# A small load moved to the head of the ACT queue, x moved to GpSimd, and the layer-norm transposes moved into those of K0

## Chip, cores, metric

One core of one Trainium2 chip. The metric is the device time of one execution in microseconds (us), lower is better. Executions of one kernel on one core are compared within rounds on the same chip; all runs quoted here are of the fast state unless said otherwise. A ratio is the mean time of one kernel's fast runs over that of the other's of the same rounds, so it is not quite the ratio of the medians that are quoted. Under 2% of difference counts as "same"; the 95% interval is given where smaller differences matter.

## The reference

A decode step: layer norm of x (2 x 576), attention over a sliding window of 2048 cached positions (32 query heads, 16 key/value heads of 128), plus a squared-ReLU MLP (576 to 4608 to 576), all added to x.

```python
x  = A_x                                    # 2 x 1 x 576, bf16
xn = _layernorm(x, axis=-1)
return x + _A_ref(xn, A_k_cache, A_v_cache, A_wq, A_wo) \
         + _B_ref(xn, B_w1, B_b1, B_w2, B_b2)
# _A_ref: q = xn @ wq; softmax(q k^T / sqrt(128)) v over the last 2048 positions; @ wo
# _B_ref: relu(xn @ w1 + b1)**2 @ w2 + b2
```

The arithmetic is small. The work is to bring 53.6 MB of K, V and weights into SBUF.

## The kernel before

All large loads are issued by the Sync engine (SP) in one queue, K0 first, then wq, then K and V blocks of 2 MB that rotate through six buffers. TensorE transposes each K block in eight groups of four matmuls; VectorE and ScalarE copy the results out in turn.

```python
x_sb = const.tile([B, D], BF16, name="x_sb")
nc.scalar.dma_start(out=x_sb[:], in_=x2d)                # x: 2 rows of 1152 B, ACT queue
# ... constants; an activation that loads the table ...
for f in issue_kv(k_tiles, A_k_cache, 0, "k"):           # K0: 128 partitions x 16 KB, SP queue
    f()
for i in range(NW):
    issue_wq(i)
# ... identity; layer norm of x_sb into xn_sb and xr_sb on VectorE and ScalarE ...
pro_ps = psum.tile([P, NXN, B], BF16, tag="misc", name="pro_ps")
for c in range(NFULL):
    pe_tr(out=pro_ps[:, c, :], in_=xn_sb[:, c:NFULL * P:NFULL], identity=ident[:B, :B])
for sg in range(S):
    pe_tr(out=pro_ps[:, NFULL + sg, :], in_=xr_sb[:, sg, :], identity=ident[:B, :B])
xnT = const.tile([P, NXN, B], BF16, name="xnT")
nc.vector.tensor_copy(out=xnT[:], in_=pro_ps[:])         # six transposes, then one copy
# ... (cut)
for g in range(NG):
    transposes(0, g)                                      # K0
for c in range(KC):
    q_block(c)                                            # uses xnT and wq
# ... scores, softmax; b1 and later b2 by GpSimd:
b2_sb = const.tile([1, D], BF16, name="b2_sb")
nc.gpsimd.dma_start(out=b2_sb[:], in_=B_b2.rearrange("(o n) -> o n", o=1))
```

## Time and profile before

| | before |
|---|---|
| time, median of 3 first runs (range) | 134.68 us (134.64 to 134.70) |
| span in the profile | 132.7 us |
| busy share TensorE / VectorE / ScalarE / GpSimd | 70% / 46% / 35% / 6% |
| bytes on the SP queue | 53.61 MB of 53.74 |
| first packet of K0; last landing of the last weights | 2.15 us; 129.19 us |

How to read it: a row of digits is the busy share of the span in 40 slices, 9 being 90% or more. "Packet records" and "landing records" below are the trace's single DMA packets and the semaphore counts they raise; the numbers in the text that no shown line carries come from there. The lines themselves are in the prediction.

### The profile page before, as it was taken

How to read it: one execution, taken by the hardware profiler on the slowest of the kernel's cores; microseconds unless marked ns; L12 is line 12 of the kernel's file. 1: busy time of each engine (PE TensorE's matmuls, PEld its weight loads, DVE VectorE, ACT ScalarE, POOL GpSimd, SP SyncE). 2: the span in 40 equal slices, each digit the busy share in tenths (PEclk: the TensorE clock that was granted, in tenths of full speed). 3: DMA queues.
4: the chain of work that ended last, by engine and by line, in shares of the span. 5: the costliest groups of instructions: out<-in, count | busy, mean ns of one | idle time of the engine just before them, and what ended most of it. 6: DMA issues, size and time to landing. Idle time of an engine off the chain costs nothing.

```text
span 132.7 us, 2060 instructions
## 1 busy us (share of the span) xinstructions
PE 92.7 (70%) x838; PEld 55.9 (42%) x838; DVE 61.2 (46%) x169; ACT 46.3 (35%) x63; POOL 7.5 (6%) x21
## 2 busy tenths in 40 slices
PE   0069456897499689688787629959937985556960
PEld 0058222673456355444444325524515942313640
DVE  6914304346533872863764772287041436443010
ACT  5717301494343274175175043412040661000010
POOL 7500000100100100100100100010000001000000
PEclk9999977779769999999999995995995599655896
DMA  4999999999999999999999999999999999999940
GB/s 159 396 412 449 415 444 415 439 420 430 437 420 444 415 449 415 439 425 434 425 415 449 420 435 433 427 433 444 417 425 430 430 434 439 406 425 434 414 203 1
DMA packets 4268, 53.74 MB, mean 405 GB/s; under 512 B 542, under 2 KB 544, under 8 KB 1060
## 3 DMA queue, kind: packets, MB, share of 16 engines
q1 hardware_dynamic: 4184, 53.61, 95.0%
q8 instruction: 6, 0.10, 0.3%
q0 software_dynamic: 64, 0.01, 0.0%
q14 instruction: 2, 0.02, 0.0%
q10 hardware_dynamic: 12, 0.00, 0.0%
HBM read 53.62 MB, written 0.00 MB: 404 GB/s over the span
## 4 chain that ended last, share of the span: by engine, by line
DMA 88%; PE 7%; SPq 3%; issue 0%; DVE 0%; DVEq 0%
DMA k<-in_A_k_cache_dram 67%; DMA w<-in_B_w_dram 21%; PE kT_ps L93 4%; SPq L111 1%; PE pv_ps L90 1%; SPq L118 1%; PE sc_ps L90 1%; SPq L123 0%; PE tail_ps L90 0%; DVE fin_sb L550 0%; PE sm L90 0%; DVEq L550 0%
## 5 line engine op out<-in xcount | busy, mean ns | idle before, releaser
L93 PE MATMUL kT_ps<-ident_f,k 128*128 128x128 f32 x256 | 43.7, 322 | 6.6 <-DMA k<-in_A_k_cache_dram 4.9
L297 ACT COPY kT<-kT_ps 128x1024 bf16<-128x1024 bf16 x32 | 31.8, 1012 | 30.1 <-PE kT_ps L93 30.1
L93 PEld LDWEIGHTS kT_ps<-ident_f,k 128*128 128x128 f32 x256 | 34.3, 165 | 18.6 <-issue 6.6
L299 DVE COPY kT<-kT_ps 128x1024 bf16<-128x1024 bf16 x32 | 22.0, 686 | 29.9 <-PE kT_ps L93 29.1
L90 PE MATMUL sc_ps<-kT,qz 128*32 128x512 bf16 x128 | 9.7, 383 | 6.2 <-DVE kT L299 5.5
L90 PE MATMUL pv_ps<-v,pT 128*32 128x512 bf16 x128 | 13.5, 467 | 0.0
L330 ACT ACTIVATE pr<-sc_ps,nb 128x512 bf16<-128x512 f32 x8 | 5.5, 687 | 20.7 <-DVE nb L327 20.7
L323 POOL PARTITION_ALL_REDUCE gmax<-m x8 | 2.9, 364 | 102.7 <-DVE m L321 80.4
L368 DVE SCALAR_TENSOR_TENSOR acc<-pv_ps,f,acc 128x128 f32<-128x128 f32 x24 | 8.3, 346 | 0.5
L90 PE MATMUL sm<-acc,tohead 128*64 128x128 f32 x16 | 4.2, 352 | 5.8 <-DVE acc L368 5.5
L332 DVE STREAM_TRANSPOSE pT<-pr 128x512 bf16<-128x512 bf16 x8 | 5.7, 709 | 5.2 <-ACT pr L330 5.2
L90 PE MATMUL out_ps<-wo,ws 128*2 128x288 bf16 x64 | 6.7, 390 | 1.1 <-DVE ws L390 1.1
L319 DVE TENSOR_REDUCE mx<-sc_ps 128x1 f32<-128x512 f32 x8 | 5.5, 692 | 3.4 <-PE sc_ps L90 3.0
L90 PEld LDWEIGHTS <-qz 128*32 128x32 bf16 x128 | 2.0, 94 | 10.0 <-DVE kT L299 7.1
L544 ACT COPY part<-out_ps 2x144 f32<-2x144 f32 x2 | 0.5, 268 | 15.0 <-DVE part L544 14.9
L90 PEld LDWEIGHTS <-ws 128*2 128x2 bf16 x64 | 3.7, 114 | 4.6 <-DVE ws L390 1.5
L90 PE MATMUL sm<-sums,samec 128*128 128x1 f32 x16 | 3.3, 276 | 3.1 <-DVE od L386 3.1
L90 PEld LDWEIGHTS sm<-acc,tohead 128*64 128x64 f32 x16 | 1.8, 161 | 8.6 <-DVE acc L368 7.9
L90 PEld LDWEIGHTS <-xnT 128*2 128x2 bf16 x100 | 2.6, 87 | 6.7 <-issue 5.5
L90 PEld LDWEIGHTS <-pT 128*32 128x32 bf16 x128 | 3.3, 102 | 4.3 <-issue 4.0
L90 PE MATMUL q_ps<-wq,xnT 128*2 128x512 bf16 x32 | 2.9, 499 | 3.2 <-DMA wq<-in_A_wq_dram 3.2
L93 PE MATMUL pro_ps<-ident,xn_sb 2*128 2x2 bf16 x4 | 0.3, 172 | 6.7 <-DVE xn_sb L198 6.7
(86 smaller groups left out, 62.3 us busy)
## 6 DMA issues: line engine op xcount, KB each, us to landing
k<-in_A_k_cache_dram SPq DMA_DIRECT2D x8, 2048.0 KB, 22.0
v<-in_A_v_cache_dram SPq DMA_DIRECT2D x8, 2048.0 KB, 27.0
wo<-in_A_wo_dram SPq DMA_DIRECT2D x2, 2304.0 KB, 23.4
w<-in_B_w_dram SPq DMA_DIRECT2D x2, 2304.0 KB, 30.9
wq<-in_A_wq_dram SPq DMA_DIRECT2D x2, 2048.0 KB, 13.9
w<-in_B_w_dram SPq DMA_DIRECT2D x3, 1296.0 KB, 27.7
w<-in_B_w_dram SPq DMA_DIRECT2D x1, 1008.0 KB, 31.8
w_rem<-in_B_w_dram SPq DMA_DIRECT2D x1, 576.0 KB, 34.2
```

What stands on the lines that cost most here:

```text
L90: return tc.keep_in_program_order(nc.tensor.matmul(out, **kw))
L93: return tc.keep_in_program_order(nc.tensor.transpose(**kw))
L111: return [lambda i=i: nc.sync.dma_start(out=tl[:, i * n:(i + 1) * n], in_=v[:, :, i * n:(i + 1) * n]) for i in range(parts)]
L118: nc.sync.dma_start(out=tl[:, 0:RW * width], in_=rows[:, i * RW * width:(i + 1) * RW * width])
L297: nc.scalar.copy(out=dst, in_=src)
L299: nc.vector.tensor_copy(out=dst, in_=src)
L319: nc.vector.tensor_reduce(out=mx[:], in_=sc_ps, axis=AX.X, op=ALU.max)
L323: nc.gpsimd.partition_all_reduce(gmax[:], m2[:], channels=P, reduce_op=ReduceOp.max)
L330: nc.scalar.activation(out=pr[:], in_=sc_ps, func=ACT.Exp, bias=nb[:], scale=scale, accum_out=sums[:])
L332: nc.vector.transpose(out=pT[:].rearrange("p t m -> p (t m)"), in_=pr[:])
L368: op = nc.vector.scalar_tensor_tensor(out=nx[:], in0=pv_ps[:, j, :], scalar=f[:, j:j + 1], in1=acc[:], op0=ALU.mult, op1=ALU.add)
L544: cp(out=part[32 * i:32 * i + B, :], in_=out_ps[32 * (i // 2):32 * (i // 2) + B, (i % 2) * OQ:(i % 2 + 1) * OQ])
```

## The change

Three moves, meant together: b2 becomes the first load on the ACT queue, in a view of 16 pieces so as to run on all 16 DMA engines; x, which had that place, goes to GpSimd, whose queue the page calls software_dynamic (software descriptors, SWDGE); since x then lands later, the six transposes of the normalised x move from ahead of K0's transposes to the middle of them.

```diff
+    b2_sb = const.tile([1, D], BF16, name="b2_sb")
+    nc.scalar.dma_start(out=b2_sb[:].rearrange("o (k n) -> o k n", k=16),
+                        in_=B_b2.rearrange("(o k n) -> o k n", o=1, k=16))
     x_sb = const.tile([B, D], BF16, name="x_sb")
-    nc.scalar.dma_start(out=x_sb[:], in_=x2d)
+    nc.gpsimd.dma_start(out=x_sb[:], in_=x2d)
 ...
-    pro_ps = ...  six pe_tr ...  xnT copy          # (before all K0 transposes)
 ...
-    for g in range(NG):
+    for g in range(NG // 2):
+        transposes(0, g)
+    pro_ps = ...  six pe_tr ...  xnT copy
+    for g in range(NG // 2, NG):
         transposes(0, g)
 ...
-    b2_sb = const.tile([1, D], BF16, name="b2_sb")
-    nc.gpsimd.dma_start(out=b2_sb[:], in_=B_b2.rearrange("(o n) -> o n", o=1))
```

More of the change, by code (lines that the diff above doesn't have):

```diff
@@ L156, in issue_w2 @@
         w2_tiles[(g, r0)] = tl
+    b2_sb = const.tile([1, D], BF16, name="b2_sb")
+    nc.scalar.dma_start(out=b2_sb[:].rearrange("o (k n) -> o k n", k=16), in_=B_b2.rearrange("(o k n) -> o k n", o=1, k=16))
     x_sb = const.tile([B, D], BF16, name="x_sb")
-    nc.scalar.dma_start(out=x_sb[:], in_=x2d)
+    nc.gpsimd.dma_start(out=x_sb[:], in_=x2d)
     eps_t = const.tile([B, 1], F32, name="eps_t")
@@ L203 @@
         nc.vector.tensor_copy(out=xr_sb[:, sg, sg::S], in_=xn_sb[:, NFULL * P:D])
-    pro_ps = psum.tile([P, NXN, B], BF16, tag="misc", name="pro_ps")
-    for c in range(NFULL):
-        pe_tr(out=pro_ps[:, c, :], in_=xn_sb[:, c:NFULL * P:NFULL], identity=ident[:B, :B])
-    for sg in range(S):
-        pe_tr(out=pro_ps[:, NFULL + sg, :], in_=xr_sb[:, sg, :], identity=ident[:B, :B])
-    xnT = const.tile([P, NXN, B], BF16, name="xnT")
-    nc.vector.tensor_copy(out=xnT[:], in_=pro_ps[:])
     own = const.tile([P, NC], F32, name="own")
@@ L490, in step @@
         softmax(u)
-    for g in range(NG):
+    for g in range(NG // 2):
+        transposes(0, g)
+    pro_ps = psum.tile([P, NXN, B], BF16, tag="misc", name="pro_ps")
+    for c in range(NFULL):
+        pe_tr(out=pro_ps[:, c, :], in_=xn_sb[:, c:NFULL * P:NFULL], identity=ident[:B, :B])
+    for sg in range(S):
+        pe_tr(out=pro_ps[:, NFULL + sg, :], in_=xr_sb[:, sg, :], identity=ident[:B, :B])
+    xnT = const.tile([P, NXN, B], BF16, name="xnT")
+    nc.vector.tensor_copy(out=xnT[:], in_=pro_ps[:])
+    for g in range(NG // 2, NG):
         transposes(0, g)
```

## The prediction

> **What bounds the kernel now.** I read the page top down first: busy shares, the slices, the queue table, the chain that ended last.
>
> ```profile
> span 132.7 us, 2060 instructions
> PE 92.7 (70%) x838; PEld 55.9 (42%) x838; DVE 61.2 (46%) x169; ACT 46.3 (35%) x63; POOL 7.5 (6%) x21
> ...
> DMA  4999999999999999999999999999999999999940
> ...
> q1 hardware_dynamic: 4184, 53.61, 95.0%
> ...
> DMA 88%; PE 7%; SPq 3%; issue 0%; DVE 0%; DVEq 0%
> ```
>
> No compute engine is above 70%, while the 16 DMA engines stand at 9 in every slice from the second to the last but two. One queue, that of the Sync engine, carries 53.61 of the 53.74 MB, and the chain is DMA for 88% of the span. Next the stretches view says at what rate that queue runs (columns: stretch, its length, busy time and instructions of each engine, granted clock, DMA share, GB/s):
>
> ```profile
> 14.00:100.00 86.00, 65.33 (x587) 37.25 (x579) 42.87 (x106) 32.92 (x46) 2.55 (x7) 0.90 1.01 430
> 100.00:127.00 27.00, 19.89 (x173) 12.62 (x173) 9.37 (x28) 4.83 (x6) 0.36 (x1) 0.68 1.00 425
> 127.00:129.00 2.00, 1.10 (x40) 0.69 (x35) 0.60 (x2) 0.54 (x2) 0.00 (x0) 1.00 0.39 158
> ```
>
> 430 GB/s in the middle, 425 later, so the stream is steady, then a ragged end. The 2 MB of one K or V block take about 4.87 us at 430 GB/s. The landing records put the 16 completions of the last weight piece between 127.33 and 129.19 us: the DMA engines end up to 1.86 us apart, and the slowest decides. The end of the chain in order of time, and the timeline there:
>
> ```profile
> 101.64 27.55 DMA w<-in_B_w_dram
> 129.19 0.04 issue
> 129.23 0.32 PE tail_ps L90 x8
> ...
> 129.65 0.31 DVE fin_sb L550
> ```
>
> So the time is: when the stream starts (first packet of K0 at 2.15 us in the packet records), plus 127.0 us of stream to 129.19, plus 3.5 us of tail to the end of the span at 132.7, plus about 2 us outside the span (134.68 measured). A change matters only if it moves one of these. Everything it touches lies at the beginning, so the last view is the timeline of the first 15 us (start, duration, engine, line, operation, idle time before and its releaser):
>
> ```profile
> 0.73 0.65 SPq L111 DMA_DIRECT2D k<-in_A_k_cache_dram  x1
> 0.73 0.56 ACTq L159 DMA_DIRECT2D x_sb<-in_A_x_dram  x1
> ...
> 1.78 0.85 POOL L501 DMA_DIRECT2D b_sb<-in_B_b_dram  x1
> ...
> 2.64 0.53 POOL L506 DMA_DIRECT2D b_sb<-in_B_b_dram  x1
> ...
> 6.66 0.29 PE L93 MATMUL pro_ps<-ident,xn_sb 2*128 2x2 bf16 x4 [6.66 <-DVE xn_sb L198]
> ...
> 8.42 3.74 PE L93 MATMUL kT_ps<-ident_f,k 128*128 128x128 f32 x20 [1.25 <-DMA k<-in_A_k_cache_dram]
> ...
> 13.95 0.54 SPq L111 DMA_DIRECT2D v<-in_A_v_cache_dram  x1
> 18.08 1.88 PE L90 MATMUL q_ps<-wq,xnT 128*2 128x512 bf16 x16 [3.20 <-DMA wq<-in_A_wq_dram]
> ```
>
> The reader should see that x, b1, b2 and the layer norm are all finished before K0 lands (8.37 us), that TensorE then works until about 14.9 and idles 3.2 us for the second half of wq.
>
> **What the Trainium skill says.** (1) "DMA: Bandwidth & Descriptors", section "Why a DMA increments its semaphore by 16 and not by 1": a copy runs on the largest number k up to 16 that divides the slowest dimension of both sides, on hardware queues the lowest-numbered k engines; on a software queue all 16 post the completion. The trace agrees: x (2 rows) left two packets of 1152 B and two of 4 B on the ACT queue. It explains the intent, because b2 viewed as 16 pieces of 36 values gets k = 16. (2) Same page, "Issuing engines are not separate DMA queues": whoever issues, the same 16 DMA engines do the work. So moving x and b2 frees no bandwidth; the 100% DMA share in the stretches agrees. (3) Same page, "Latency and other measured facts": first byte after about 0.6 us by hardware descriptors, about 1 us by software. Here x's first packet came 0.93 us after its issue began, but b1's 4.39 us after (6.17 against 1.78) behind a full stream, and b1 and b2 landed 6.4 and 6.3 us after issue. The measured 6.3 is what I use for x. (4) "SBUF — State Buffer", section "SBUF: two separate sides": some VectorE modes keep GpSimd from writing software descriptors. x's descriptors will be written at about 0.7 to 1.6 us, while VectorE does its memsets. The b1 issue took 0.85 us against 0.53 for b2, which may or may not be that; it can delay x by tenths.
>
> **The change part by part.**
>
> *b2 from GpSimd to the head of ACT.* 1152 B. In the packet records b2 was already 16 data packets of 72 B at about 12 ns; the bytes and their spread over engines stay. GpSimd loses an issue of 0.53 us that nobody waited for. ACT keeps one issue, 0.56 us in x's place, at most 0.65 as for 16-engine issues on SP, before a table load that starts at 1.33. On the path to the end: 0, unless the descriptors of b2 (16 data plus 16 completions instead of 2 plus 2) delay those of K0, issued in the same instant. SP issues a load with 16 x (8 + 1) = 144 packets every 0.57 us (wq0 to wq1), so 28 more cost by estimate at most 28/144 x 0.57 = 0.11 us. Against it, all 16 engines rather than two will have been touched before K0: the first K0 packets took 0.67 to 0.95 us against some 0.61 later, so there is at most about 0.2 us to win. I put the sum at 0, plus or minus 0.2.
>
> *x from ACT to GpSimd.* x landed at 2.05 and VectorE first read it at 3.06. Now it is GpSimd's first instruction, at about 0.72. If it behaves like b1, it lands near 0.72 + 6.3 = 7.0; issued before the stream fills the engines it could be 3 to 5. GpSimd's memsets and b1 shift by 0.85 less 0.53, about 0.3 us; nobody is near them.
>
> *The layer norm.* In the built kernel VectorE's order now has the second q memset (0.48) and ident_f ahead of the first statistics, so the identity that K0's transposes need does not wait for x, ready near 3.7 as before or a few tenths later. Behind the wait for x are, with their durations: statistics 0.45 and 0.44, ident 0.20, own 0.31, aggregate 0.19, own_j 0.26, offm 0.21, own_s 0.33, qhead 0.37, sel 0.20, reciprocal 0.09, xn 0.42, xr 0.30: 3.8 us. From 7.0 that gives 10.8. The six transposes now come after four of the eight K0 groups, whose last ended near 11.7 in before (VectorE starts its copy of group 3 at 11.76). 10.8 is earlier, so TensorE does not wait; one K0 copy due on VectorE at 10.42 waits 0.4. x could land as late as 11.7 - 3.8 = 7.9 with no stall.
>
> *The six transposes on TensorE.* 0.29 + 0.28 = 0.57 us, from idle time into the run of K0 transposes, with a copy of 0.17 on VectorE. K0's last transpose ends near 14.5 in place of 13.9. Two consequences: the q work waits for wq1 anyway (3.2 us idle, minus 0.6 to 1.0, still over 2 us), so q and everything behind it are unmoved; and the load of V2, which waits for K0's buffer, is issued at about 14.5 in place of 13.95. The DMA queue then holds work until K3 lands at 44.6 us, so it cannot notice. The smallest distance anywhere between an issue on SP and the landing of the load ahead of it is 13.6 us (V3 issued at 40.87, K4 landed at 54.49).
>
> *Sum.* Stream start 0 +- 0.2; stream rate and bytes 0; tail 0 (the output stores already run on both queues, 129.98 and 129.99). Expected 134.6 us, a difference of -0.1 that I would not defend against 0.
>
> **The rivals.** (a) *x comes so late that TensorE stands still.* The 6.3 us of b1 and b2 speak for it; an even longer wait of the first software load is possible. If x landed at 10, xr would be ready at 13.8, TensorE would idle 2 us in the middle of K0 and finish at 16.5. The q work still waits until 18.08 for wq1, and the queue has 13.6 us or more in hand: the time stays 134.6. Only x later than about 12 would move q, and then the K1 step has slack again. (b) *The stream starts earlier or later, by the descriptor work of b2 or by already touched engines.* For it: x's first packet was at 1.66 and K0's only at 2.15, though both were issued at 0.73. It makes 134.2 to 134.9. (c) *The ragged end evens out.* If the small loads of x on two engines caused it, spreading b2 would win up to 1 us (slowest 129.19 against a middle of about 128.3 in the landing records): 133.7. Against: x's packets took 0.055 and 0.060 us, and early loads land within 0.6 us of each other (K0: 7.83 to 8.37), the gap appears only after 27 us, when the first 16 KB instruction fetch of 0.88 us runs on that queue. Six such fetches remain. (d) *A later TensorE loses its clock at the end.* The page grants 0.5 to 0.6 in the last third; TensorE finishes its part at 127.66, about 0.9 us before the weights it waits for. A shift of the throttled stretches could cost 0.5 to 1: 135.4. I see no reason for the first 15 us to do this.
>
> **Range and chances.** Most likely 134.6. (b) gives +-0.3, runs on another chip some 0.3% (0.4 us), (c) and (d) the tails: 134.0 to 135.1 in 8 of 10. Faster by 2% needs 2.7 us; all bytes at 430 GB/s take 124.7 us of the 127.0, so even a perfect stream gives only 2.3, hence 1%. Slower by 2% needs the DMA to run dry or the throttle to hit the end, 2%.
>
> **What would show each step.** Right: K0's first packet within 0.2 us of 2.15; x landing between 3 and 8 with the first statistics right after; the six transposes between the fourth and fifth K0 group near 11.7 without a long wait for xn; V2 issued at about 14.5; 430 GB/s in the same middle stretch; the ACT queue with 40 packets (16 + 16 + 8) instead of 12; the last weights landing at 129 +- 0.4. Wrong: a last landing that moved by over 0.5 us, completions of it noticeably closer together, or a gap in the DMA row. The prediction fails most plainly if the start of the stream moves by more than 0.3 us, since nothing downstream would hide or undo that.

## The result

The changed kernel took 134.73 us (median of 6, 134.67 to 134.83) against 134.69 (6 runs, 134.63 to 134.99). The ratio is 0.9999, 95% interval 0.9986 to 1.0011: the same, inside the predicted range and 0.13 us from the predicted 134.6.

The profile after, in the order of the prediction's views. The page's lines first: span, queue of SP and ACT, and the chain by engine.

```profile
span 133.0 us, 2060 instructions
...
q1 hardware_dynamic: 4184, 53.61, 94.8%
...
q10 hardware_dynamic: 10, 0.00, 0.0%
...
DMA 89%; PE 5%; SPq 2%; issue 0%; DVE 0%; DVEq 0%
```

The same bound, the same bytes. K0's first packet is at 2.150 us in the packet records, against 2.149. One line is not as predicted: the ACT queue (q10) has 10 packets, not 40. The stretches of the changed kernel (same columns as before):

```profile
14.00:100.00 86.00, 64.39 (x591) 36.77 (x591) 43.14 (x107) 33.44 (x47) 2.55 (x7) 0.90 1.01 430
100.00:127.00 27.00, 19.50 (x163) 12.19 (x163) 9.37 (x28) 4.83 (x6) 0.36 (x1) 0.68 1.00 426
```

430 and 426 GB/s, against 430 and 425. The end of its chain in order of time:

```profile
101.85 27.57 DMA w<-in_B_w_dram
129.42 0.04 issue
129.46 0.32 PE tail_ps L90 x8
```

129.42 in place of 129.19; it is at the edge of the predicted 129 +- 0.4, and since the medians of all runs differ by 0.04 us, I take this 0.2 for scatter between executions. Then the timeline of the start, where everything moved:

```profile
0.73 0.52 ACTq L159 DMA_DIRECT2D b_sb<-in_B_b_dram  x1
...
1.25 0.85 POOL L161 DMA_DIRECT2D x_sb<-in_A_x_dram  x1 [0.81 <-POOLq L569]
...
7.14 0.45 DVE L192 BATCH_NORM_STATS2 stats<-x_sb 2x6 f32<-2x288 bf16 x1 [3.19 <-DMA x_sb<-in_A_x_dram]
...
9.83 0.30 DVE L205 COPY xr_sb<-xn_sb 2x64 bf16<-2x64 bf16 x2
...
12.14 0.29 PE L93 MATMUL pro_ps<-ident,xn_sb 2*128 2x2 bf16 x4
...
14.86 0.54 SPq L111 DMA_DIRECT2D v<-in_A_v_cache_dram  x1
...
18.15 1.15 PE L90 MATMUL q_ps<-wq,xnT 128*2 128x512 bf16 x16 [2.36 <-DMA wq<-in_A_wq_dram]
```

x lands 5 us later than before (7.12 against 2.05) and VectorE stands still 3.19 us for it. The transposes find xn ready, as no idle time stands in front of them. V2 is issued 0.9 us later (14.86 against 13.95). And all of it ends in the same place: q waits for the second half of wq until 18.15 in place of 18.08, its wait having shrunk from 3.20 to 2.36 us.

### The profile page after: what moved, and what is told of

It is laid out like the page before. It is cut to its first block, busy times and chain, and to the rows that moved or that the text cites. A ratio compares the mean times of both kernels' runs of the same rounds, so it can differ in the third digit from the quotient of the medians.

```text
span 133.0 us, 2060 instructions
## 1 busy us (share of the span) xinstructions
PE 91.5 (69%) x838; PEld 55.1 (41%) x838; DVE 61.1 (46%) x169; ACT 46.3 (35%) x63; POOL 7.1 (5%) x21
## 4 chain that ended last, share of the span: by engine, by line
DMA 89%; PE 5%; SPq 2%; issue 0%; DVE 0%; DVEq 0%
DMA k<-in_A_k_cache_dram 68%; DMA w<-in_B_w_dram 21%; PE kT_ps L93 3%; SPq L111 1%; PE pv_ps L90 1%; SPq L118 1%; PE sc_ps L90 1%; SPq L123 0%; PE tail_ps L90 0%; DVE fin_sb L552 0%; PE sm L90 0%; DVEq L552 0%
## 5 line engine op out<-in xcount | busy, mean ns | idle before, releaser
L90 PE MATMUL sc_ps<-kT,qz 128*32 128x512 bf16 x128 | 10.5, 414 | 6.0 <-DVE kT L293 5.5
L90 PE MATMUL pv_ps<-v,pT 128*32 128x512 bf16 x128 | 12.9, 445 | 0.0
L90 PE MATMUL out_ps<-wo,ws 128*2 128x288 bf16 x64 | 6.0, 360 | 1.1 <-DVE ws L384 1.1
L90 PEld LDWEIGHTS sm<-sums,samec 128*128 128x128 f32 x16 | 2.8, 219 | 3.7 <-DVE od L380 2.3
L415 DVE TENSOR_TENSOR hrow<-t 98x384 bf16<-98x384 f32 x3 | 1.6, 556 | 5.2 <-ACT t L414 5.0
```

The lines of the kernel that those rows point to most:

```text
L90: return tc.keep_in_program_order(nc.tensor.matmul(out, **kw))
L415: nc.vector.tensor_tensor(out=hrow[:, k * HB:(k + 1) * HB], in0=t1, in1=t1, op=ALU.mult)
```

## The experiments

The theory: the time is the start of SP's stream, its bytes at its rate, and a tail; what else happens in the first 15 us is hidden behind a queue that is 13 us or more ahead. Rivals: (A) a gain from the ACT queue's head and a loss from x's late landing cancel; (B) the ACT issue of the same instant holds K0 back; (C) nothing was won only because b2 was in fact not spread; (D) TensorE's lateness is felt. Twelve kernels in three groups; each ran beside the kernel before on its group's chip (medians of before in those groups: 134.72, 134.67, 134.81). All gave correct results.

### 1. b2 back to GpSimd, nothing on ACT (e1_act_empty)

```diff
-    nc.scalar.dma_start(out=b2_sb[:].rearrange(...), in_=B_b2.rearrange(...))   # head of ACT
+    nc.gpsimd.dma_start(out=b2_sb[:], in_=B_b2.rearrange("(o n) -> o n", o=1))  # at its old place
```

> The changed kernel with b2 back on GpSimd, so that ACT issues nothing before the end. Theory (the time is the start of the Sync queue's stream, its bytes, and the tail; what else happens in the first 15 us is hidden): 134.7 us, within 0.2% of before, K0's first packet at 2.15 +- 0.1 us. Rival A (a gain and a loss cancel: the ACT queue's head helps the stream, x's late landing costs the same): without the ACT issue only the loss is left, so 0.3 us or more slower than before. Rival B (the ACT issue of the same instant holds K0's descriptors back): first packet at about 1.66 us and a time 0.4 to 0.5 us lower.

Measured: 135.00 us, ratio 1.0015 (1.0003 to 1.0028); K0's first packet at 2.25. Rival B falls: with nothing else issued, K0 did not start earlier. Rival A asked for 0.3 us or more; 1.5 parts in a thousand are 0.2 us, too near to it to refuse A by this run alone, so experiment 2 tests A from the other side.

### 2. b2 alone moved (e11_b2_only)

```diff
+    nc.scalar.dma_start(out=b2_sb[:].rearrange(...), in_=B_b2.rearrange(...))
     nc.scalar.dma_start(out=x_sb[:], in_=x2d)      # x stays on ACT, behind b2
 ...
-    nc.gpsimd.dma_start(out=b2_sb[:], in_=B_b2.rearrange("(o n) -> o n", o=1))
```

> The kernel before with b2 alone moved to the head of ACT and x behind it on ACT; x stays on its hardware queue and the transposes at their place. Theory of the stream: 134.7 within 0.2%, K0's first packet at 2.15 +- 0.15, x landed by 2.6 us. Rival A (a gain of the ACT part cancelled by x's late landing in the full change): now the gain alone, 134.4 or lower.

Measured: 134.79, ratio 0.9999 (0.9985 to 1.0012); K0's first packet at 2.16. There is no gain for a loss to cancel: A falls. The expectation missed x, which now sat behind K0 in the DMA engines: its packets came at 3.81 us, not before 2.6. It was hidden all the same.

### 3. The transposes back in front of K0 (e3_early_tr)

```diff
+    pro_ps = ...  six pe_tr ...  xnT copy          # ahead of all K0 transposes again
-    pro_ps = ...  six pe_tr ...  xnT copy          # between groups 3 and 4
```

> The changed kernel with the six layer-norm transposes put back ahead of all K0 transposes. Theory: TensorE now waits for xn until about 10.2 us, K0's transposes start 1.7 us later than in the changed kernel and V2 is issued near 16; the time stays 134.7, within 0.2%, since the queue holds work until 44 us. Rival D (the later issue of loads is felt): slower by 1 us or more.

Measured: 134.74, ratio 0.9996 (0.9985 to 1.0008). TensorE waits for xn, and the loads behind K0's buffer go out later still:

```profile
9.87 0.29 PE L93 MATMUL pro_ps<-ident,xn_sb 2*128 2x2 bf16 x4 [9.87 <-DVE xn_sb L200]
...
16.52 0.54 SPq L111 DMA_DIRECT2D v<-in_A_v_cache_dram  x1
```

V2 goes out 2.6 us later than in the kernel before, and no time is lost. So the third part of the change was not needed for the time either.

### 4. x about 13 us later (e4_late_x_a)

```diff
+    for i in range(11):                            # the one memset of qz further on is taken out
+        tc.keep_in_program_order(nc.gpsimd.memset(qz[:], 0.0))
+    tc.keep_in_program_order(nc.gpsimd.tensor_copy(out=x_sb[:], in_=<zeros of qz>))
     nc.gpsimd.dma_start(out=x_sb[:], in_=x2d)
```

> The changed kernel with eleven extra GpSimd memsets ahead of the issue of x, so that x lands at about 20 us in place of 7.1. Theory: VectorE and so TensorE stand still until then, K0's transposes end near 30 us in place of 14.8 and V2 is issued then, but the queue holds work until 44.6 us; the steps behind it are delayed by about 7 us and catch up: 134.7 us, within 0.3% of before. Rival D (a late TensorE is felt at once): slower by 5 us or more.

Measured: x landed at 20.42 and V2 was issued at 26.49. The profiled execution took 134.68 us and another 134.67, both the time of before. But the other four took 135.21, 136.47, 135.57 and, of the slow state, 137.51, with no relation to the granted clock (0.936, 0.873, 0.919, 0.857) that I could read; the ratio of the fast ones is 1.0061 (1.0024 to 1.0097). So 12.5 us of lateness can be absorbed, and are not always. What the slower executions lost is open: none of them left a profile, and in the profiled one no load was issued on SP less than 8.5 us before the load ahead of it had landed (V4 at 55.69, K5 at 64.23).

### 5. x about 35 us later (e5_late_x_b)

The same edit with 32 memsets.

> The same with 32 extra memsets: x lands at about 40 us, K0's buffer comes free near 50 us, after the last load in the queue (K3, 44.6 us). Theory: now the slack is used up, the DMA row shows a gap of 5 to 10 us near 45 to 55 us and the time rises by about as much, to 140 to 148 us. If the time stays at 134.7 the theory of the stream as the bound is wrong.

Measured: 153.56, ratio 1.14. The queue ran dry, as these two rows of its page and two stretches show (last columns DMA share and GB/s):

```profile
DMA  5999999999920930969999999999999999999910
GB/s 199 396 432 424 424 424 454 428 419 428 437 104 0 398 160 2 393 259 424 424 290 376 437 419 434 432 428 440 409 431 441 415 437 431 417 431 429 394 59 3
```

```profile
45.00:55.00 10.00, 8.18 (x90) 5.43 (x89) 3.62 (x8) 3.08 (x6) 0.00 (x0) 1.00 0.54 211
55.00:65.00 10.00, 8.41 (x79) 5.46 (x77) 6.15 (x17) 7.88 (x10) 0.72 (x2) 1.00 0.45 171
```

K3, the last load in the queue, had landed at 43.56, and V2 could be issued only at 48.17, when K0's transposes were done. The direction is the theory's. The size is not: 19 us lost where 5 to 13 were expected. There was not one gap but a series, since each later load now waited for TensorE to free its buffer (0 GB/s from 45 to 49 us, 2 from 57 to 61, 290 near 78; a slice is 3.8 us). The slack is real and it has an end.

### 6. x first on the SP queue (e6_x_on_sp)

```diff
-    nc.scalar.dma_start(out=x_sb[:], in_=x2d)
+    nc.sync.dma_start(out=x_sb[:], in_=x2d)
```

> The kernel before with x issued on the Sync queue ahead of K0. K0's issue then begins 0.5 to 0.7 us later. Theory: the stream starts that much later and nothing gives it back: K0's first packet at 2.6 to 2.8, time 135.2 to 135.4 us, 0.4% to 0.5% slower. If the start of the stream is not a term of the time: 134.7.

Measured: 135.21, ratio 1.0041 (1.0029 to 1.0053), that is 0.55 us.

```profile
0.72 0.35 SPq L159 DMA_DIRECT2D x_sb<-in_A_x_dram  x1
1.14 0.63 SPq L111 DMA_DIRECT2D k<-in_A_k_cache_dram  x1
```

K0's issue begins 0.41 us later (1.14 against 0.73), its first packet 0.39 later (2.54), its landing 0.62 later (8.99). The start of the stream is a term of the time and nothing returns it, though the expected delay of the packet was a little too large. This is a load of 2304 B whose place costs more than anything the change moved.

### 7. More bytes in the stream (e7_more_bytes)

```diff
     load_k(1)
+    nc.sync.dma_start(out=<dummy: 128 x 2048 bf16>, in_=<part of K1>)   # 0.52 MB nobody reads
     load_v(0)
```

> The kernel before with a load of 0.52 MB that nobody reads put into the Sync queue early. Theory: 0.52 MB at 430 GB/s are 1.2 us, and the time rises by that to 135.9 us (0.9%). If something other than the bytes of the stream sets the end: less than 0.3 us.

Measured: 135.96, ratio 1.0099 (1.0086 to 1.0112): 1.3 us for 1.2 expected. The bytes of the stream are the second term.

### 8. b2 really in 16 pieces (e2_b2_16)

In the changed kernel the ACT queue's first load is one packet of 1152 B at 1.64 us and one completion. The view of 16 x 36 contiguous values had been merged back into one run of 576 while building (the built program has it so), and the run went out as one packet. A tile with a gap after each piece cannot be merged:

```diff
-    b2_sb = const.tile([1, D], BF16, name="b2_sb")
-    nc.scalar.dma_start(out=b2_sb[:].rearrange("o (k n) -> o k n", k=16), in_=...)
+    b2_sb = const.tile([1, 16, 48], BF16, name="b2_sb")
+    nc.scalar.dma_start(out=b2_sb[:, :, 0:D // 16], in_=...)
 ...                                                    # its reader takes the pieces; so in 9 and 10
```

> The changed kernel with b2 in a padded tile (16 pieces at a step of 48 values), so that the load cannot be merged into one run of 1152 B and goes out in 16 pieces of 72 B. Theory: 134.7 us, within 0.2% of before; the ACT queue shows 40 packets (16 + 16 + 8) in place of 10, K0's first packet within 0.15 us of 2.15. Rival C (the change won nothing only because b2 was in fact not spread, one packet on one engine): with the spread real, K0's first packets are shorter (0.61 to 0.7 us in place of 0.71 to 0.98) or start earlier, and the time falls by 0.2 to 0.5 us.

Measured: 135.63, ratio 1.0066 (1.0053 to 1.0079): 0.9 us slower, which no theory had expected.

```profile
q10 hardware_dynamic: 40, 0.00, 0.0%
```

```profile
14.00:100.00 86.00, 62.63 (x582) 34.90 (x582) 42.65 (x107) 33.38 (x47) 2.56 (x7) 0.92 1.01 428
```

The first of these lines is from its queue table, the second from its stretches (428 GB/s for 430). The 40 packets are there, 16 of 72 B. K0's first packet is unmoved (2.155), its first packets are no shorter (0.86 to 1.03 us), and the pieces came at 4.99 us, behind K0's. Rival C falls: the spread as intended would have won nothing. The loss sits in the whole stream. From the first completion of wq0 to the first of the last weight piece take 114.74 us in before and 114.77 in the changed kernel, 115.41 here. Two new theories: the second hardware queue, once used on all 16 engines, slows the first; or the larger tile did it, for it moved every large tile in SBUF by 384 B.

### 9. and 10. The layout without the queue, and the queue without the layout (e9_shift_only, e10_b2_16_512)

```diff
# 9, on the kernel before: b2 stays on GpSimd at its old place
+    b2_sb = const.tile([1, 16, 48], BF16, name="b2_sb")     # 1536 B: large tiles at 384 mod 512
# 10, on the changed kernel: 16 pieces on ACT
+    b2_sb = const.tile([1, 16, 52], BF16, name="b2_sb")     # 1664 B: large tiles at 0 mod 512
```

> The kernel before, with b2 left on GpSimd at its old place but in the padded tile of 1536 B, so that every large tile lies 384 B higher in SBUF (at 384 modulo 512 in place of 0). Two theories for the 0.9 us that the run with b2 in 16 pieces lost. Layout (rows that begin off a multiple of 512 B are written a little slower, all through the stream): 135.5 to 135.7, 2 MB each 4.895 us in place of 4.868. Queue (a second hardware queue once used on all 16 DMA engines slows the first): 134.7, 4.868 us.

> The changed kernel with b2 in 16 pieces on ACT as in the run that lost 0.9 us, but at a step of 52 values, so that the tile grows by 512 B and every large tile stays on a multiple of 512 B. Layout: 134.7 within 0.2%, 4.868 us per 2 MB. Queue: 135.5 to 135.7, 4.895 us. In both, 16 packets of 72 B on the ACT queue.

Measured: 9 takes 135.57, ratio 1.0053 (1.0041 to 1.0066), and 115.36 us for the stretch of the stream named above; 10 takes 135.00, ratio 1.0011 (0.9998 to 1.0023), and 114.77 us, with its 16 packets of 72 B on the ACT queue. The stretch of the middle, of 9 and then of 10:

```profile
14.00:100.00 86.00, 65.63 (x587) 37.81 (x585) 42.88 (x106) 33.27 (x47) 2.55 (x7) 0.88 1.01 427
```

```profile
14.00:100.00 86.00, 67.19 (x589) 38.14 (x589) 43.31 (x107) 33.45 (x47) 2.55 (x7) 0.86 1.01 429
```

The layout does it, the queue does not. In the built programs the large tiles begin at a multiple of 512 B in before, in the changed kernel and in 10, and 384 B past one in 8 and 9; this costs 0.6 us in 115, 0.5%. The stretch repeats well: in 1, 2, 3 and 12, with the tiles unshifted, it takes 114.76 to 114.77 us. No other offset was tried, so which multiple matters is not shown. The Trainium skill, "DMA: Bandwidth & Descriptors", section "How a descriptor splits into AXI transactions", says that a descriptor moves in transactions of 256 B and that one that starts off such a boundary begins with a partial one. It would fit, since 384 B past a multiple of 512 is 128 B past one of 256: a 16 KB row would take 65 in place of 64, by estimate 1.6%, of which a third is seen here. The page's account is of reads, and these are writes, so the mechanism is a likeness and not shown; that the address matters is shown. A change of 384 B in one small tile thus costs more than the change under study could ever win.

### 11. K0 in two loads by partitions (e8_k0_split)

```diff
-    for f in issue_kv(k_tiles, A_k_cache, 0, "k"): ...
+    ...
+    nc.sync.dma_start(out=k0[0:32, :],  in_=kv0[:, 0, :])
+    nc.sync.dma_start(out=k0[32:P, :], in_=kv0[:, 1:TH, :])
```

> The kernel before with K0 in two loads, its first 32 partitions and then the other 96, so that the first load has 16 x (2 + 1) packets in place of 16 x (8 + 1). Theory: the start of the stream is one of the three terms of the time; if K0's 0.5 us later start against x (2.15 against 1.66) is time for making its descriptors, the first packet comes at 1.7 to 1.9 and the time falls by 0.2 to 0.5 us to 134.2 to 134.5. If the start is a fixed latency, first packet at 2.15 and 134.7, or up to 0.2 us slower by the smaller loads.

Measured: 140.68, ratio 1.0443. The half that was tested came out as hoped: the first packet is at 1.747 in place of 2.149, so K0's later start against x goes with the number of its packets (48 here, 144 before). That the time is spent on making their descriptors is the likely reading. What the expectation did not contain is the rate between 2 and 13 us, first before, then this kernel:

```profile
2.00:13.00 11.00, 4.91 (x32) 4.56 (x33) 6.21 (x24) 6.62 (x9) 3.12 (x7) 1.00 1.00 411
```

```profile
2.00:13.00 11.00, 0.51 (x6) 0.40 (x6) 4.83 (x22) 3.89 (x6) 3.14 (x7) 1.00 0.93 221
```

The DMA engines are as busy (0.93) at half the rate: 190 GB/s over 11 us are 2.1 MB, 4.9 us at 430. Many packets of 16 KB took 1.1 to 1.25 us in place of 0.61. The completions of the last piece lie 3.2 us apart in place of 1.9. These two, less the 0.4 us won at the start, make 5.8 of the 6.0 us lost by this estimate; in the profiles the last landing moved by 5.5 (134.70 for 129.19).

### 12. K0 in two loads by columns (e12_k0_cols)

```diff
-    for f in issue_kv(k_tiles, A_k_cache, 0, "k"):
+    for f in issue_kv(k_tiles, A_k_cache, 0, "k", parts=2):
```

> The kernel before with K0 in two loads by columns, each over all 128 partitions (control for the split by partitions, which started the stream 0.4 us earlier and then lost 6 us). If the count of packets sets the start: the first load has 144 packets again, first packet at 2.15. If the split by partitions, not the second load, cost the rate: no loss of rate between 2 and 13 us (about 411 GB/s), time 134.7 to 134.9.

Measured: 134.93, ratio 1.0009 (0.9996 to 1.0021), first packet at 2.16, 406 GB/s from 2 to 13 us:

```profile
2.00:13.00 11.00, 6.33 (x35) 6.29 (x36) 6.69 (x25) 6.90 (x9) 3.13 (x7) 1.00 1.01 406
```

So a second load costs nothing and wins nothing; the split by partitions cost the rate. And with 144 packets again, of 8 KB, the first load starts as late as a load of twice its bytes: the start goes with the count and not with the bytes. A cause that fits is told by the Trainium skill, "DMA: Bandwidth & Descriptors", section "The descriptor swizzle": in a transfer over 128 partitions each engine writes its own SBUF port. With 32 and 96 partitions the shares fall otherwise, and packets of twice the length are what two engines on one port would show. That is argued. The landing and packet records of 11 fit it: the slow packets end with K0. Its second part completes between 10.41 and 14.20 us, 3.8 us apart, and the packets that start after 14 us take 0.61 us again, those of wq0, a load of 128 partitions, among them.

None of the twelve beats the two kernels; the only one with an earlier stream, number 11, lost far more later.

## Why the prediction was right

**The bound.** Right, and now shown from four sides: later start (6: +0.55 us), more bytes (7: +1.3 us), a slower rate (9: +0.76 us of median), and lateness of the compute engines that costs nothing at 2.6 us (3), something in three of five fast executions at 12.5 us (4), and 19 us once the queue runs dry (5). The tail was not varied.

**b2.** The cost, 0, was right. The step under it was wrong: "16 data plus 16 completions" and "the ACT queue with 40 packets". The queue left 10: b2 was one packet on one engine, merged while building. Experiments 8 and 10 show that it did not matter: with the 40 packets real and the layout kept, the time is unmoved. The allowance of 0.2 us for touched engines was not used either, since the 16 pieces ran only after K0 had begun (3.14 us in 10).

**x.** Landed at 7.12 for 7.0 predicted, by two errors that cancel: GpSimd began the issue at 1.25, not 0.72, and the landing took 5.87 us after that, not 6.3. The stall of VectorE, 3.19 us, was expected and hidden.

**Layer norm.** xr was ready at 10.13 for 10.8: neighbouring VectorE instructions of this chain mostly overlap, by 0.06 to 0.09 us each, so the sum of their durations was too long. The transposes began at 12.14 for 11.7 without waiting.

**V2.** Issued at 14.86 for 14.5, 0.9 us late in place of 0.55; the K0 run began 0.14 later and its copies were packed less well. Hidden, as experiment 3 shows with 2.6 us.

**One reading.** Not all small loads were finished before K0, as the prediction says: b2 landed at 8.92 us, by the prediction's own 2.64 + 6.3, and K0 at 8.37. Nothing hung on it, since b2 is first read at 32.9.

**Rival (a).** Its claim that x later than about 12 us would still be absorbed is only partly borne out: at 20.4 us two of six executions kept the time (experiment 4).

**Rival (c), the ragged end.** It did not even out: the completions of the last piece lie 1.86 us apart before, 2.00 after. The landing records of before support what the prediction gave as the cause. Completions more than 1 us behind the first, by load, beside the instruction fetches that the packet records show on the DMA engines:

```
load's first completion   28.4  38.2  52.7  67.3  88.0  99.7  124.2  (us)
late completions of 16       1     2     3     4     5     6      7
fetch before it           27.0  33.8  49.6  63.6  83.9  99.1  124.1
```

In this profile each fetch makes one more late engine, and a late engine stays late. (The fetch at 33.8 us is of 8 KB, the others of 16; another of 8 KB at 79.6 left an engine 0.8 us late. The 16 KB ones are on a queue of their own, q8, and not on that of the loads, as the prediction has it.) No experiment removed a fetch, but two moved it, and the lateness moved with it. In 4 the first fetch comes at 35.0 us, and the first load with a late completion is that of 38.3; those of 28.6 and 33.4 have none. In 5 the fetch at 55.0 fell at the end of V2 with nothing queued behind it and left none, and the one at 73.5 left one in the load of 77.7. This makes the fetches the likely cause of the first late engines, not of all: later in 5 as many as 9 were late.

**Rival (d), the clock at the end.** It did not come about: the granted clock from 100 to 127 us is 0.68 in both profiles. TensorE did finish its part later, at 128.33 (start and duration of its last group in the timeline) in place of 127.62, but it still waited 0.43 us for the last weights (0.90 before).

## What to carry to other kernels

When one queue of loads sets the time, sort every move into one of four: does it shift the start of the queue, its bytes, its rate, or the tail? If into none, it is worth nothing however many waits it takes away, as long as the queue is far enough ahead; how far, a deliberate delay tells. Check in the built program or the packet records that a view meant to spread a load survived the build, and after every new tile that the large tiles still begin where they did.

## What the Trainium skill lacked or had wrong

- "DMA: Bandwidth & Descriptors", "Why a DMA increments its semaphore by 16 and not by 1": it says that software can split a contiguous run so that it sprays. Here the plain run of 1152 B went out as 16 packets of 72 B from GpSimd, and as one packet from ACT, though the kernel gave it there as a view of 16 x 36; a gap after each piece was needed to keep 16 on ACT. The page doesn't say that a contiguous view can be undone.
- Same page, "Latency and other measured facts": about 1 us to the first byte by software descriptors. In this kernel x's first packet came 4.37 us after its issue began, b1's 4.39 (before), and the landings took 5.9 and 6.4 us, beside a stream that fills the engines. By hardware, x took 0.93 us for about 0.6.
- No page has the start of a hardware load against its number of packets: 4 packets 0.93 us from issue to first packet, 48 packets 1.02, 144 packets 1.42.
- "How a descriptor splits into AXI transactions", same page: reads only. For tiles written 384 B past a multiple of 512 B the runs show 115.36 and 115.41 us in place of 114.74 to 114.77, 0.5%.
- "SBUF — State Buffer", "SBUF: two separate sides": the traces gave no sign of VectorE holding up software descriptors. In 4 and 5 VectorE stood still from 12.9 us until x landed, x was issued at 15.0 and 36.1, and its first packet still came 3.6 us after that. The first load issued by GpSimd took 0.85 us and the second 0.52 to 0.53, whether b1 was first or x. No page has that difference.
- "Runtime: NRT & Kernel Launch", "Instruction fetch mechanics", has instruction fetches in blocks of 16 KB, but neither it nor another page has what they do to a stream of loads: six of them took 0.88 to 0.97 us each, one more engine was late after each, and the completions lay 1.9 us apart at the end.
